# A pre-LN transformer block on one core: transposes of the second LayerNorm placed later, weights of the last block loaded in another order

## The chip, the cores and the metric

The kernel runs on one core of one Trainium2 chip. The metric is the device time of one execution in microseconds (us). A profiled execution is a separate run; its own time stands beside its span below.

## The reference

The inputs are `x` [1, 2048, 512] and the weights, all float32. What is computed, cut to the core:

```python
def A(x, wq, wk, wv, wo):            # 32 query heads of 16, one key/value head
    q = (x @ wq).reshape(B, S, 32, 16).transpose(0, 2, 1, 3)
    k, v = x @ wk, x @ wv
    p = softmax(einsum("bhqd,bkd->bhqk", q, k) * 16 ** -0.5)
    o = einsum("bhqk,bkd->bhqd", p, v)
    return o.transpose(0, 2, 1, 3).reshape(B, S, 512) @ wo

def B(x, w_gate, w_up, w_down):      # 512 -> 1792 -> 512
    return (gelu(x @ w_gate) * (x @ w_up)) @ w_down

h  = x + A(layernorm(x), wq, wk, wv, wo)
h2 = h + B(layernorm(h), w_gate, w_up, w_down)
```

## The kernel before

**Tiling.** The 2048 rows are four blocks of 512 (`NB = 4`, `T = 512`), each of four tiles of 128 rows (`TB = 4`). float32 operands are split into a high and a low part (`hi`, `lo`), and a product is the three terms high-high, high-low and low-high. A prologue normalizes `x` and makes keys, values and the first queries. Then a loop runs over block, group of four heads and key chunk: `scores` (L343) makes two heads' scores on TensorE and their exps `p` on ScalarE, and `weigh` (L356) multiplies exps by values into `acc`. A set of weighings that stand together is a "run of V" (move `v`). `p` tiles live in five buffers (`PB = 5`).

**Weaving.** From a little into block 1 on, the dense work of the block before is woven between the scores: the output projection `pp`, the second LayerNorm, its transposes `pxt`, the gate and up products `pg` and `pu`, and the down products `pd`. These products run on halves of 64 rows, two at a time, in three PSUM banks that `take_bank` hands out in turn (`spare`). The order of TensorE, GpSimd and ScalarE is as written out everywhere (a manual schedule); in the woven part that of VectorE and of the SP queue too. A table of moves, `CYCLES`, gives each round: first `before`, then `finish(count)`, which issues a run of V, then scores (`s`), dense steps (`d`) and further V (`v`). A counter `clock` counts one for each score and dense step and four for each `v`.

**The second LayerNorm.** When a tile's `pp` is done, `norm` (L549) takes the statistics on VectorE (L130, L131) and GpSimd (L133, L134), and `scale` writes the normalized rows `xb` (L554) and notes the clock in `scaled_at`. `before` (L1039) issues a tile's transposes (`turn`, L570) when the clock is `LAG = 6` past that. `turn` makes four TensorE transposes into a PSUM bank (L575), two copies to `x2h` and `x2l` on VectorE (L583, L584), and the load of a later row of `x` into the freed `xb` buffer (L514). The first gate product of a block waits until four tiles are turned.

**Weights.** The split gate and up weights lie in DRAM as `w1`, 512 KB for one product, and go through three buffers; `load_w1` (L493) asks for the one three ahead. The split down weights `w2` come in tiles of 1 MB, seven to a block, also in three buffers (`load_w2`, L502). Both are issued on the SP queue.

**The last block.** `last_dense` (L788) does block 3's dense work with nothing woven beside it, whole products of 12 matmuls at L772. It takes three `p` buffers for `x`, the normalized rows and `h` (`xp`, `xn`, `h`; loads at L810). The last heads' output goes through DRAM: `oT` is copied from `acc` (L371), stored to `acc_d` (L372), loaded to `oc` (L382), and `piece` (L400) divides it on VectorE (L387, L404) ahead of the last quarter of `pp` (L825). `rest` (L777) holds two down products of block 2 as filler between the steps. Behind this, `up` (L863) asks for two `w1` after both of its products, and the loop over `RUNS` asks for two `w2` at the first feature chunk of each run. In this part only the order of TensorE, GpSimd and ScalarE is written out; a scheduler places the DMAs of the SP queue.

Of the kernel before, what the change touches and what calls it, by code (L numbers as in the profile page):

```python
# [10 lines left out]
F32R = mybir.dt.float32r  # L11
# [8 lines left out]
P = 128  # L20
# [6 lines left out]
PB = 5  # L27
# [11 lines left out]
SUMS = ((0, 1, 2, 3), (4, 5, 6, 7), (8, 9, 10, 11, 12, 13))  # L39

LAG = 6

CYCLES = (
    (3, "ssdddddsdddsddds", "vssvssvs"),
# [11 lines left out]
def kernel(  # L56
# [19 lines left out]
    T = 512  # L76
# [77 lines left out]
    def run(outer, first):  # L154
# [271 lines left out]
                pieces[b] = TB  # L426

        late = ExitStack()
        db = None

        def part_weights(pw):

# [67 lines left out]
            w1s[b, f, k] = w  # L500

        def load_w2(b, j):  # L502
            w = db.tile([P, 2, 2, D], F32R, tag="w2", bufs=3, name=f"w2_{b}_{j}")
            nc.sync.dma_start(
                w.bitcast(F32), w2_d[2 * j : 2 * j + 2].rearrange("f p i d -> p f i d").bitcast(F32)
            )
            w2s[b, j] = w
# [10 lines left out]
        tanhs, later = [], []  # L518
        clock = 0

        def prime():
            for i in range(3):
                load_x(i)
                load_w1(i)
            for j in range(3):
                load_w2(0, j)
# [13 lines left out]
        def project(b, t):  # L540
            def terms():
                o_hi, o_lo = o_blk[b]
                sl = slice(t * P, (t + 1) * P)
                return product_terms([
                    (None, (o_hi[:, c, sl], o_lo[:, c, sl]), (wo_hi[:, c, :], wo_lo[:, c, :]))
                    for c in range(DC)
                ])

            def norm():  # L549
                x = xbs[b, t]  # L550
                scaled = layer_norm(db, x, hs[b, t], f"2_{b}_{t}")

                def scale():
                    scaled()  # L554
                    scaled_at[b, t] = clock

                later.insert(min(1, len(later)), scale)

            def done(a, bank):
                if a == 0:  # L560
                    h = db.tile([P, D], F32, tag="h", bufs=6, name=f"h_{b}_{t}")
                    nc.vector.tensor_tensor(h, bank, xbs[b, t], op=ALU.add)
                    hs[b, t] = h
                else:
                    nc.vector.tensor_tensor(hs[b, t], hs[b, t], bank, op=ALU.add)
                    later.append(norm)

            return f"pp_{b}_{t}", 3 * DC, terms, done, lambda: pieces.get(b, 0) > t

        def turn(b, t):  # L570
            tag, bank = take_bank(f"pxt_{b}_{t}")
            pt = bank.rearrange("p (c q) -> p c q", c=DC)
            xn = xbs.pop((b, t))
            for c in range(DC):
                nc.tensor.transpose(pt[:, c, :], xn[:, c * P : (c + 1) * P], ident)  # L575
            if t == 0:
                xTs[b] = [
                    db.tile([P, DC, T], F32R, tag=f"x2{w[0]}", bufs=1, name=f"x2{w[0]}_{b}")
                    for w in ("hi", "lo")
                ]  # L580
            sl = slice(t * P, (t + 1) * P)
            hi, lo = (x[:, :, sl] for x in xTs[b])
            nc.vector.tensor_copy(hi, pt)  # L583
            nc.vector.tensor_tensor(lo, pt, hi.bitcast(F32), op=ALU.subtract)  # L584
            spare.append(tag)
            load_x(b * TB + t + 3)
            turned[b] = t + 1
# [200 lines left out]
        def last_dense():  # L788
            b = NB - 1
            o_hi, o_lo = o_blk[b]  # L790
            xns, hb = {}, {}
            xT_hi = db.tile([P, DC, T], F32R, tag="x2h", bufs=1, name=f"x2h_{b}")
            xT_lo = db.tile([P, DC, T], F32R, tag="x2l", bufs=1, name=f"x2l_{b}")

            def x_turn(t):
                pt = tail_bank(f"pxt_{b}_{t}").rearrange("p (c q) -> p c q", c=DC)
# [11 lines left out]
            )  # L808
            for t in range(TB):
                nc.sync.dma_start(xp[:, t, :], x_t[:, b * TB + t, :])  # L810

            pps = [psum1(f"pp_{b}_0")]
            pps.extend(tail_bank(f"pp_{b}_{t}") for t in range(1, TB))
# [14 lines left out]
                    )  # L828

            def norm(t):  # L830
                scaled[t] = layer_norm(db, xns[t], pps[t], f"2_{b}_{t}", on_act=True)

            piece, scaled = last_out.pop(), {}
            for t in range(TB):
# [26 lines left out]
                nc.scalar.activation(hb[t], pps[t], AF.Copy)  # L861

            def up(f, gh, gl):  # L863
                terms = []
                for k in range(2):
                    w = w1s.pop((b, f, k))
                    terms.append(
                        [(w[:, i, c, :], xT_hi[:, c, :]) for c in range(DC) for i in range(2)]
                        + [(w[:, 0, c, :], xT_lo[:, c, :]) for c in range(DC)]
                    )  # L870
                pg, pu = yield from solo([f"pg_{b}_{f}", f"pu_{b}_{f}"], terms)
                g = db.tile([P, T], F32, tag="g", bufs=2, name=f"g_{b}_{f}")
                nc.vector.tensor_copy(g, pg)
                a = db.tile([P, T], F32, tag="ga", bufs=2, name=f"ga_{b}_{f}")
                nc.vector.tensor_tensor(a, g, g, op=ALU.mult)
                nc.vector.scalar_tensor_tensor(  # L876
                    a, a, 1.0 / GELU_A, g, op0=ALU.add, op1=ALU.mult
                )
                nc.scalar.activation(a, a, AF.Tanh, scale=GELU_A * GELU_C)  # L879
                nc.vector.scalar_tensor_tensor(a, a, 1.0, g, op0=ALU.add, op1=ALU.mult)  # L880
                nc.vector.tensor_tensor(a, a, pu, op=ALU.mult)
                split(nc.vector, gh[:, f % 2, :], gl[:, f % 2, :], a)
                for k in range(2):
                    load_w1(b * 2 * FC + 2 * f + k + 3)

            def down(fs, last):
                for t0 in range(0, TB, 2):
# [20 lines left out]
            for fs in RUNS:  # L908
                early_f = 2 if fs is RUNS[-1] else 1
                for n, f in enumerate(fs):  # L910
                    if f % 2 == 0:
                        gs[b, f // 2] = [
                            db.tile([P, 2, T], F32R, tag=tag, bufs=3, name=f"{tag}_{b}_{f // 2}")
                            for tag in ("gh", "gl")
                        ]
                    yield from up(f, *gs[b, f // 2])
                    if fs is RUNS[-1] and n == 0:
                        load_w2(b, f // 2)
                    if n + 1 == early_f and prev is not None:
                        yield from down(prev, False)  # L920
                    if fs is not RUNS[-1] and n + 1 == early_f:
                        for g in fs[::2]:
                            load_w2(b, g // 2)
                prev = fs
            yield from down(prev, True)

# [48 lines left out]
        with tc.manual_schedule(engines={mybir.EngineType.SP, mybir.EngineType.DVE}):  # L975
            parts = None
            if first:
                work = later_q()
                parts = part_weights(early.enter_context(tc.tile_pool(name="parts", bufs=1)))


            normed = True

            def visit():
                nonlocal work, normed
                total, k = 0, None
                while work is not None and total < 6 and (k != 2 or last == 0):
                    last, k = k, next(work, None)
                    if k is None:
                        work = None  # L990
                        return
                    total += k
                normed = k != 4

            def norm():
                nonlocal normed
                if not normed:
                    next(work)
                    normed = True

            def pace():
                nonlocal n, parts, db
                if n == 2 * PER:
                    drain()
                    for _ in parts or ():
                        pass
                    parts = None
                    early.close()
                    db = late.enter_context(tc.tile_pool(name="dense", bufs=1))
                score(n)  # L1010
                n += 1
                if n % 4:
                    return
                if outs:
                    take_out()
                if parts is not None and n > 12 and n % 24:
                    next(parts, None)
                if n == 2 * PER + 4:
                    prime()

            moves = {"s": pace, "p": visit, "n": norm, "v": partial(finish, 1)}
            for move in OPENING + PERIOD * (PER // KC):
                moves[move]()
            while n < lead:
                pace()
                if n % 4 == 2 and len(pend) > 2 and n < lead - 1:
                    finish(1)
                elif n % 4 == 0:
                    finish(len(pend) - 2)
# [9 lines left out]
        def before(idle):  # L1039
            if outs:  # L1040
                take_out()
            while (b_t := divmod(sum(turned.values()), TB)) in scaled_at:
                if clock - scaled_at[b_t] < LAG:
                    break
                turn(*b_t)
                if not idle:
# [378 lines left out]
```

## Time and profile before

| | |
|---|---|
| time, median of 3 runs | 1445.45 us (1445.38 to 1445.54) |
| the profiled execution: its own time, its span | 1446.27 us, 1444.3 us |
| TensorE matmul (PE) busy | 1397.6 us |
| ScalarE (ACT) busy | 1031.0 us |
| VectorE (DVE) busy | 640.4 us |
| GpSimd (POOL) busy | 218.7 us |
| granted TensorE clock, mean | 0.998 |
| moved by DMA | 180.57 MB |

All times in the profile are in us from the first instruction, so the span lies a little under the execution's time. PE is the matmul row and PEld the weight loads, which overlap it. A row of the timeline has start, length, engine, line, operation, output and input tiles and the count of merged instructions; in brackets stands the idle time of that engine just before and what ended it. A row of the waits has the waiting engine and line, the releaser, the sum, the number of times and the longest. A row of the windows has the stretch and its length, then busy time and instructions of PE, PEld, DVE, ACT and POOL, the granted TensorE clock, the busy share of the 16 DMA engines and GB/s. The chain is the work that ended last, followed back from the end. SPq is the queue of DMAs that the sync engine issues.

### The profile page before, as it was taken

What the parts mean: (1) busy time and instruction counts of PE and PEld (TensorE: products, weight loads), DVE (VectorE), ACT (ScalarE), POOL (GpSimd) and SP (SyncE); (2) the same over time, 40 slices, a digit from 0 to 9 for tenths busy, and PEclk for the clock granted to TensorE, in tenths of its full rate; (3) what the DMA queues carried; (4) which work ended last, traced back from release to release, by engine and by line L of the source; (5) the groups of instructions that cost most, each with busy time, mean ns of one, the idle gap of its engine ahead of it and who ended that gap; (6) DMA issues with size and microseconds to landing.
All of it is one profiled execution on the core that took longest, in us unless ns stands there. A gap on an engine that the chain in (4) does not pass through costs nothing.

```text
span 1444.3 us, 25110 instructions
## 1 busy us (share of the span) xinstructions
PE 1397.6 (97%) x10384; PEld 754.3 (52%) x10384; DVE 640.4 (44%) x1043; ACT 1031.0 (71%) x1147; POOL 218.7 (15%) x305
## 2 busy tenths in 40 slices
PE   6999999999999999998999999998999999999998
PEld 5433333334455555554555555544555555567776
DVE  7413131223364444554354544545264453546665
ACT  7699999996878777785777777786778777752000
POOL 5577778601000000000000000000000000001000
PEclk9999999999999999999999999999999999999999
DMA  4467667633222333211422323211323323224552
GB/s 155 144 212 220 222 222 245 208 133 132 78 95 75 118 100 114 100 56 58 169 82 78 129 100 114 100 49 40 139 93 100 114 99 113 90 88 175 188 176 76
DMA packets 66930, 180.57 MB, mean 125 GB/s; under 512 B 9436, under 2 KB 9436, under 8 KB 66776
## 3 DMA queue, kind: packets, MB, share of 16 engines
q1 hardware_dynamic: 56976, 144.79, 29.8%
q0 software_dynamic: 9760, 34.08, 7.1%
q8 instruction: 84, 1.38, 0.4%
q14 instruction: 38, 0.31, 0.1%
q10 hardware_dynamic: 72, 0.00, 0.0%
HBM read 131.13 MB, written 47.71 MB: 124 GB/s over the span
## 4 chain that ended last, share of the span: by engine, by line
PE 86%; DVE 6%; ACT 3%; DMA 2%; issue 1%; POOL 1%; SPq 0%; ACTq 0%; DVEq 0%; POOLq 0%
PE acc L358 31%; PE s L350 19%; PE pg L742 8%; PE pd L742 7%; PE pu L742 6%; PE pq L203 3%; PE pd L772 3%; ACT p L354 3%; PE pu L772 2%; PE pg L772 2%; PE pp L742 2%; DMA w<-w_d 1%; PE pd_rest L784 1%; DVE st L130 1%; PE pxt L575 0%
## 5 line engine op out<-in xcount | busy, mean ns | idle before, releaser
L354 ACT ACTIVATE p<-s 128x1024 f32<-128x1024 f32 x1024 | 960.5, 1040 | 254.5 <-PE s L350 254.2
L358 PE MATMUL acc<-p,v_sb 128*32 128x512 f32 x4096 | 491.6, 600 | 0.0
L350 PE MATMUL s<-qg,kaug 50*128 50x512 f32 x1984 | 388.2, 426 | 4.1 <-ACT p L354 3.5
L350 PEld LDWEIGHTS s<-qg,kaug 50*128 50x128 f32 x1984 | 171.5, 184 | 284.1 <-issue 133.8
L358 PEld LDWEIGHTS acc<-p,v_sb 128*32 128x32 f32 x4096 | 110.2, 109 | 231.3 <-issue 215.9
L742 PE MATMUL pg<-x2h,w 64*128 64x512 f32 x672 | 177.4, 394 | 4.2 <-DVE g L616 3.1
L742 PE MATMUL pu<-x2h,w 64*128 64x512 f32 x672 | 175.3, 394 | 0.0
L133 POOL TENSOR_SCALAR rstd<-mv 128x1 f32<-128x1 f32 x16 | 3.5, 220 | 989.7 <-DVE mv L131 956.8
L742 PE MATMUL pd<-w,gh 64*128 64x512 f32 x624 | 124.9, 394 | 1.4 <-DVE h L672 1.4
L672 DVE TENSOR_TENSOR h<-h,pd 128x512 f32<-128x512 f32 x80 | 54.3, 685 | 151.7 <-PE pd L742 151.7
L742 PEld LDWEIGHTS pg<-x2h,w 64*128 64x128 f32 x672 | 96.1, 186 | 20.5 <-DVE g L616 6.6
L742 PE MATMUL pg<-x2l,w 64*128 64x512 f32 x336 | 100.7, 392 | 0.0
L742 PEld LDWEIGHTS pu<-x2h,w 64*128 64x128 f32 x672 | 94.3, 186 | 11.2
L742 PE MATMUL pu<-x2l,w 64*128 64x512 f32 x336 | 99.2, 392 | 0.0
L879 ACT ACTIVATE ga<-ga 128x512 f32<-128x512 f32 x14 | 8.9, 632 | 94.5 <-DVE ga L876 94.5
L742 PEld LDWEIGHTS pd<-w,gh 64*128 64x128 f32 x624 | 68.9, 186 | 12.8 <-DVE h L672 2.7
L742 PE MATMUL pd<-w,gl 64*128 64x512 f32 x312 | 72.1, 392 | 0.0
L387 DVE RECIPROCAL oc<-oc 128x128 f32<-128x128 f32 x64 | 56.6, 922 | 32.0 <-DMA oc<-acc_d 31.9
L616 DVE TENSOR_TENSOR g<-g,pg 128x512 f32<-128x512 f32 x42 | 28.8, 685 | 91.1 <-PE pg L742 91.1
L616 DVE TENSOR_TENSOR u<-u,pu 128x512 f32<-128x512 f32 x42 | 28.9, 688 | 78.9 <-PE pu L742 78.7
L612 DVE COPY g<-pg 128x512 f32<-128x512 f32 x42 | 29.0, 691 | 74.2 <-PE pg L742 74.2
L123 DVE CAST qh<-pq 128x512 fp32r<-128x512 f32 x11 | 7.6, 689 | 110.1 <-PE pq L203 110.1
(242 smaller groups left out, 1479.2 us busy)
## 6 DMA issues: line engine op xcount, KB each, us to landing
w<-w_d SPq DMA_DIRECT2D x112, 512.0 KB
w<-w_d SPq DMA_DIRECT2D x28, 1024.0 KB
qg<-q_d SPq DMA_DIRECT2D x62, 200.0 KB
q_d<-qh SPq DMA_DIRECT2D x32, 256.0 KB
acc_d<-oT SPq DMA_DIRECT2D x32, 256.0 KB
oc<-acc_d SPq DMA_DIRECT2D x128, 64.0 KB
w_d<-w_0b POOLq DMA_DIRECT2D x14, 512.0 KB, 3.6
w_d<-w_1b POOLq DMA_DIRECT2D x14, 512.0 KB, 5.2
```

Of the source, the lines that this page charges most:

```text
L130: nc.vector.bn_stats(st, src)
L203: nc.tensor.matmul(pq, wt[:, d, c * P : (c + 1) * P], xt[:, d, :], start=(n == 0), stop=(n == 3 * DC - 1),)
L350: nc.tensor.matmul(s[:, a, :], kaug[rows, kc * P : (kc + 1) * P], qg[rows, u, :], start=True, stop=True,)
L354: nc.scalar.activation(p[:, 2 * u : 2 * u + 2, :], s, AF.Exp, scale=SCALE)
L358: nc.tensor.matmul(acc[32 * j : 32 * j + 32, :], v_sb[:, kc, :], p[:, j, :], start=(kc == 0), stop=(kc == KC - 1), skip_group_check=True,)
L387: nc.vector.reciprocal(oc[:, 1, sl], oc[:, 1, sl])
L612: nc.vector.tensor_copy(half, bank)
L616: nc.vector.tensor_tensor(half, half, bank, op=ALU.add)
L672: nc.vector.tensor_tensor(hs[b, t], hs[b, t], bank, op=ALU.add)
L742: nc.tensor.matmul(bank, lhsT[r], rhs[r], start=(k == 0), stop=(k == n - 1), skip_group_check=True,)
L772: nc.tensor.matmul(bank, lhsT, rhs, start=(i == 0), stop=(i == len(ts) - 1))
L784: nc.tensor.matmul(bank, lhsT, rhs, start=(i == 0), stop=(i == len(ts) - 1))
```

## The change

- The transposes wait for `SETTLE = 14` counts of the clock behind the scaling, where they waited for `LAG = 6`. `LAG` also sets how far the second half of the rows runs behind the first; that stays at 6.
- In the last block, `load_w1` is called after each of the two products of a chunk instead of twice after both.
- In the last block, the first two `w2` tiles lie in the two `p` buffers that are free there, and are asked for right behind the loads of `x`. The other five are asked for behind chunks 1, 2, 5 and 8.
- `x2h` and `x2l` of block 0 are allocated ahead of the other dense tiles, and the small tiles of the LayerNorm in a pool of their own (`tiny`) behind them, so that the dense tiles have other places in SBUF.

```diff
+SETTLE = 14
...
         def load_w2(b, j):
-            w = db.tile([P, 2, 2, D], F32R, tag="w2", bufs=3, name=f"w2_{b}_{j}")
+            if b == NB - 1 and j < 2:
+                w = sb.tile([P, 2, 2, D], F32R, tag="p", bufs=PB, name=f"w2_{b}_{j}")
+            else:
+                w = db.tile([P, 2, 2, D], F32R, tag="w2", bufs=3, name=f"w2_{b}_{j}")
...
+        def new_xT(b):
+            xTs[b] = [
+                db.tile([P, DC, T], F32R, tag=f"x2{w[0]}", bufs=1, name=f"x2{w[0]}_{b}")
+                for w in ("hi", "lo")
+            ]
+
         def prime():
+            new_xT(0)
...
-                scaled = layer_norm(db, x, hs[b, t], f"2_{b}_{t}")
+                scaled = layer_norm(tiny, x, hs[b, t], f"2_{b}_{t}")
...
             for t in range(TB):
                 nc.sync.dma_start(xp[:, t, :], x_t[:, b * TB + t, :])
+            for j in range(2):
+                load_w2(b, j)
...
             def up(f, gh, gl):
-                terms = []
+                banks = []
                 for k in range(2):
                     w = w1s.pop((b, f, k))
-                    terms.append(
-                        [(w[:, i, c, :], xT_hi[:, c, :]) for c in range(DC) for i in range(2)]
-                        + [(w[:, 0, c, :], xT_lo[:, c, :]) for c in range(DC)]
-                    )
-                pg, pu = yield from solo([f"pg_{b}_{f}", f"pu_{b}_{f}"], terms)
+                    terms = [(w[:, i, c, :], xT_hi[:, c, :]) for c in range(DC) for i in range(2)]
+                    terms += [(w[:, 0, c, :], xT_lo[:, c, :]) for c in range(DC)]
+                    banks += yield from solo([f"p{'gu'[k]}_{b}_{f}"], [terms])
+                    load_w1(b * 2 * FC + 2 * f + k + 3)
+                pg, pu = banks
...
-                for k in range(2):
-                    load_w1(b * 2 * FC + 2 * f + k + 3)
...
-                    if fs is RUNS[-1] and n == 0:
-                        load_w2(b, f // 2)
                     if n + 1 == early_f and prev is not None:
                         yield from down(prev, False)
-                    if fs is not RUNS[-1] and n + 1 == early_f:
-                        for g in fs[::2]:
-                            load_w2(b, g // 2)
+                    for j in {1: (2,), 2: (3,), 5: (4,), 8: (5, 6)}.get(f, ()):
+                        load_w2(b, j)
...
                     db = late.enter_context(tc.tile_pool(name="dense", bufs=1))
+                    tiny = late.enter_context(tc.tile_pool(name="tiny", bufs=1))
...
             while (b_t := divmod(sum(turned.values()), TB)) in scaled_at:
-                if clock - scaled_at[b_t] < LAG:
+                if clock - scaled_at[b_t] < SETTLE:
                     break
```

More of the change, by code (lines that the diff above doesn't have):

```diff
@@ L428, in run @@
         late = ExitStack()
-        db = None
+        db = tiny = None
         def part_weights(pw):
@@ L575, in turn @@
                 nc.tensor.transpose(pt[:, c, :], xn[:, c * P : (c + 1) * P], ident)
[L576 to L580, printed above, removed]
+            if b not in xTs:
+                new_xT(b)
             sl = slice(t * P, (t + 1) * P)
@@ L791, in last_dense @@
             xns, hb = {}, {}
-            xT_hi = db.tile([P, DC, T], F32R, tag="x2h", bufs=1, name=f"x2h_{b}")
-            xT_lo = db.tile([P, DC, T], F32R, tag="x2l", bufs=1, name=f"x2l_{b}")
+            new_xT(b)
+            xT_hi, xT_lo = xTs[b]
             def x_turn(t):
@@ L830, in norm @@
             def norm(t):
-                scaled[t] = layer_norm(db, xns[t], pps[t], f"2_{b}_{t}", on_act=True)
+                scaled[t] = layer_norm(tiny, xns[t], pps[t], f"2_{b}_{t}", on_act=True)
             piece, scaled = last_out.pop(), {}
@@ L1001, in pace @@
             def pace():
-                nonlocal n, parts, db
+                nonlocal n, parts, db, tiny
                 if n == 2 * PER:
```

## The prediction

> **What bounds the kernel now.** I read the page first (busy shares, chain by line), then the busy time by stage, then the waits and the order of time around the steps that the change moves.
>
> ```profile
> span 1444.3 us, 25110 instructions
> PE 1397.6 (97%) x10384; PEld 754.3 (52%) x10384; DVE 640.4 (44%) x1043; ACT 1031.0 (71%) x1147; POOL 218.7 (15%) x305
> PE 86%; DVE 6%; ACT 3%; DMA 2%; issue 1%; POOL 1%; SPq 0%; ACTq 0%; DVEq 0%; POOLq 0%
> 500.00:700.00 200.00, 194.05 (x1612) 105.52 (x1608) 93.20 (x151) 148.61 (x162) 3.12 (x8) 1.00 0.26 86
> 700.00:900.00 200.00, 198.22 (x1650) 108.42 (x1644) 94.92 (x144) 152.39 (x167) 0.00 (x0) 1.00 0.33 113
> 900.00:1100.00 200.00, 191.59 (x1564) 102.27 (x1564) 93.35 (x153) 147.38 (x162) 3.12 (x8) 1.00 0.27 91
> ```
>
> TensorE sets the time: 97% busy, 86% of the chain. In the middle, where attention scores and dense products are woven, ScalarE has a quarter of its time free (152 of 200 us), VectorE half. The stretch 700 to 900 loses 1.8 us of TensorE; the stretches with a second LayerNorm (500 to 700, 900 to 1100) lose 6.0 and 8.4. So the LayerNorm costs TensorE something, and what it costs stands in the wait in front of the transposes `pxt`.
>
> ```profile
> who waited for it (us, times):
>   PE pxt L575: 13.8, 10
> 339.83 0.66 PE L575 MATMUL pxt<-ident,xb 128*128 128x128 f32 x4 [2.13 <-DVE xb L554]
> 357.31 0.66 PE L575 MATMUL pxt<-ident,xb 128*128 128x128 f32 x4
> 983.13 0.66 PE L575 MATMUL pxt<-ident,xb 128*128 128x128 f32 x4 [1.54 <-DVE h L562]
> 998.55 0.40 PE L350 MATMUL s<-qg,kaug 50*128 50x512 f32 x2
> 999.98 0.55 DVE L554 TENSOR_SCALAR xb<-h,mv,rstd 128x512 f32<-128x512 f32 x1 [0.99 <-POOL rstd L134]
> 1000.58 0.66 PE L575 MATMUL pxt<-ident,xb 128*128 128x128 f32 x4 [1.64 <-DVE xb L554]
> 1003.57 5.60 ACT L354 ACTIVATE p<-s 128x1024 f32<-128x1024 f32 x6 [3.40 <-PE s L350]
> 1004.02 0.69 DVE L562 TENSOR_TENSOR h<-pp,xb 128x512 f32<-128x512 f32 x1 [0.17 <-PE pp L742]
> 1005.70 0.69 DVE L565 TENSOR_TENSOR h<-h,pp 128x512 f32<-128x512 f32 x1 [0.99 <-PE pp L742]
> 1008.92 0.66 PE L575 MATMUL pxt<-ident,xb 128*128 128x128 f32 x4 [0.90 <-DVE xb L554]
> PEld acc L358 <- ACT p L354: 14.1, 50, 0.3
> L358 PE MATMUL acc<-p,v_sb 128*32 128x512 f32 x4096 | 491.6, 600 | 0.0
> ```
>
> The rows are in order of time, with the idle time ahead of an instruction and what ended it in brackets. The normalized rows `xb` are ready at 1000.53, 1.6 us after the last scores ahead of the transposes, and TensorE, whose order is written out, stands still. That adds up to 13.8 us in ten of the twelve tiles, 0.90 to 2.13 each.
>
> **Part 1: the transposes one run of V later.** Nothing is added or removed. In the built order of the changed kernel each `pxt` of tile t stands where that of tile t+1 stood (in block 0, tiles 1 and 2 stand together, and tile 3 stays); no other TensorE instruction moves, so no round without dense work is added. The new place is about 8.4 us further on (1000.58 to 1008.92), and `xb` is written then. What else could hold the transposes there? Their PSUM bank: of three, two are in the running products and the transpose takes the third. At the place of 1008.92 this is the bank that the addition at 1005.70 has emptied by 1006.4; the wait on `h` at 983.13, which is a wait for a bank, was at a place that no transpose has any more. VectorE's two copies behind each transpose move with it; it has half its time free. The next product takes another bank, and the first gate product comes a round after the last transpose. On the SP queue the load of a row of `x`, issued behind each transpose, moves to behind a store of `oT`, four loads of `oc`, two of `qg` or a store of `h`, which therefore come no later. One such load is needed soon, that of tile 3 of the same block: it is now issued at about 992 in place of 984, and its reader is the addition at 1004.02.
>
> So the whole 13.8 us can go: a transpose without a wait costs its 0.66 us and no gap (357.31). What is late next is ScalarE: V runs now begin earlier against the exps. The weighings are 4096 matmul records, at 24 a run (three weighings, the most that stand together) 171 runs. 14.1 us of waits for exps over 171 runs is 0.08 us a run, for the ten runs that lose their stall 0.8 us. I take 13.8 - 0.8 = **13.0 us gained**. ScalarE idles 3.40 us behind such a place, so it is no new bound. Bounds: 10 if each of the ten meets the longest wait of that row, 0.3 us, and keeps a little of its own; 14.5 if the pipeline's refill behind each stall goes too.
>
> **Part 2: weights of the last block.** Asking for `w1` product by product changes nothing: before, too, each load already waited for its own product only, and the queue order of the `w1` loads is the same. What moves is `w2`: tiles 0 and 1 go into two `p` buffers that the V run at 1280.83 frees, in the SP queue behind `xp`; so tiles 2, 3, 4 take the places that 0, 1, 2 had, and the two loads that were issued together at 1355.93 vanish from there. The pair at 1390.54 stays.
>
> ```profile
> 1323.26 0.43 SPq L504 DMA_DIRECT2D w<-w_d  x1
> 1355.93 1.77 SPq L504 DMA_DIRECT2D w<-w_d  x2
> 1390.54 1.75 SPq L504 DMA_DIRECT2D w<-w_d  x2
> 1360.13 6.31 DMA w<-w_d
> 1366.57 3.02 PE pu L772 x12
> 1369.59 2.79 PE pg L772 x12
> PE pu L772 <- DMA w<-w_d: 2.3, 3, 1.1
> ```
>
> At 1360.13 a `w1` load needs 6.31 us because 2 MB of `w2` lie ahead of it; two products cover 5.6. TensorE ends the waiting product at 1369.59; without the wait it would end three products of 2.79 behind 1360.13, at 1368.5. So **1.1 us gained**. The other two of the three waits keep their causes, `w2` loads at 1323.26 and 1390.54, and remain. Bounds: 0, and 3.0 if all three went: 2.3 in the last row, and 0.2 each for the product that starts slowly (3.02 in place of 2.79).
>
> **Part 3: what the early `w2` tiles stand in front of.** This is the cost. The new SP order is `xp`, `w2` tile 0, two stores of `h`, `w2` tile 1, and only then the last store of `oT` and the loads of `oc`, which everything at the end hangs on.
>
> ```profile
> 1280.83 2.78 PE L358 MATMUL acc<-p,v_sb 128*32 128x512 f32 x24
> 1281.99 1.76 SPq L810 DMA_DIRECT2D xp<-in_A_x_dram  x4
> 1289.76 1.37 SPq L674 DMA_DIRECT2D out_dram<-h  x2
> 1292.68 2.06 DMA acc_d<-oT
> 1296.06 2.25 DMA oc<-acc_d
> 1298.49 0.95 DVE L387 RECIPROCAL oc<-oc 128x128 f32<-128x128 f32 x1 [5.84 <-DMA oc<-acc_d]
> 1306.21 0.50 PE L825 MATMUL pp<-wo_hi,o_hi 128*128 128x512 f32 x1 [0.21 <-DVE o_hi L123]
> 1317.00:1319.00 2.00, 2.00 (x11) 1.60 (x10) 0.69 (x1) 0.83 (x2) 0.00 (x0) 1.00 1.01 383
> ```
>
> Tile 0 is issued right behind `xp`, at 1283.8, and is through before the store at 1292.68 (`xp` and it, 2 MB, are 5.5 us at the 383 GB/s of the last row). Tile 1 stands behind the stores of `h`, issued until 1289.76 + 1.37 = 1291.1, so it goes 1.5 us ahead of the `oT` store. Its 1 MB takes 2.7 us at that rate, of a stretch in which such loads ran; the store's data then wait 2.7 - 1.5 = 1.2 us in the same 16 queues, and I add 0.6 us because the load starts behind the `h` stores. So `oc`, the pieces on VectorE and the last projection come 1.8 us later; TensorE waits for the pieces (0.21 at 1306.21), so there is no slack: **1.8 us lost**. Bounds: 0.5, if the load gets ahead in the pause before the store, and 5.5, if tile 0 too is late and 1 MB + 0.5 MB + 1 MB lie ahead (2.6 MB at 383 GB/s is 6.8 us, less 1.5 of lead, rounded up for their starts).
>
> The Trainium skill ("DMA: Bandwidth & Descriptors", "Anatomy of one DMA") says that DMA engines do not wait on semaphores, they just consume their queues, which speaks against this part; by its fit of 2 us plus bytes over 436 GB/s, 1 MB would hold the queue 2.4 us, and the loss would be an estimated 1.5 us.
>
> **Part 4: order of tiles in SBUF.** No instruction changes, and no row of the trace tells one place in SBUF from another, so I cost the move at 0, with -0.5 and +0.5 as bounds. The early loads of block 0 still lie on buffers whose readers end before 315.
>
> **Sum.** -13.0 - 1.1 + 1.8 = -12.3. The profiled execution took 1446.27 us (span 1444.3 and 2.0 around it), 0.8 above the median 1445.45 of unprofiled runs: 1434.0 profiled, **1433.2 us** as a run.
>
> **Rivals.**
> *The stall moves instead of going.* The V runs, now earlier, wait for exps, or the copies behind a transpose hold the next bank. For it: a stall lets ScalarE catch up. Against it: ScalarE idles 3.40 us right behind. If half the gain is lost, 1433.2 + 6.5 = 1439.7; if all, 1446.2, which is no change.
>
> *The `oT` store is held for longer.* 5.5 us in place of 1.8, and TensorE idle for that long drops its clock. The trace has one such drop:
>
> ```profile
> 304.00:308.00 4.00, 3.05 (x24) 0.93 (x16) 1.37 (x4) 3.86 (x6) 1.28 (x4) 1.00 0.10 24
> 308.00:312.00 4.00, 3.88 (x18) 0.78 (x19) 0.00 (x0) 2.82 (x4) 0.00 (x0) 0.59 0.17 62
> 303.73 1.92 PE L358 MATMUL acc<-p,v_sb 128*32 128x512 f32 x16
> 308.55 3.52 PE L358 MATMUL acc<-p,v_sb 128*32 128x512 f32 x16
> ```
>
> The same 16 matmuls took 3.52 in place of 1.92 us, so a drop costs 1.6. That gives 1433.2 + 3.7 + 1.6 = 1438.5. The Trainium skill ("TensorE: Matmul & The Clock Gate", "Part 1: The HAM clock gate") puts the drop behind an idle window of about 3.4 us; the drop above came behind a stretch that was 76% busy, so the trace is the stricter one.
>
> *Slower: the `oT` store behind slow loads.* The same place with another price. All that stands ahead of the store from 1283.8 on, 2.6 MB, would have to move at the rate that the queues show there today:
>
> ```profile
> 1285.00:1291.00 6.00, 5.46 (x40) 3.25 (x41) 3.25 (x5) 3.02 (x4) 0.00 (x0) 1.00 0.31 102
> ```
>
> At 102 GB/s it is through at 1309.5, and the store, whose data would have started near 1293.6, is 15.9 us late; with one drop of the clock, 1433.2 - 1.8 + 15.9 + 1.6 = 1448.9. It decides from a delay of 14.1 us (110 GB/s) with no drop, and the change is slower by over 0.2% from 17.0 us, or 15.4 with a drop. Against it: the 102 GB/s are what was asked for, with the engines 31% busy; where more was asked for they moved 383.
>
> *It doesn't do what it says.* For `w1` this is so (part 2). For the transposes the built order shows the move.
>
> **Chances.** Forecast 0.74; stall half kept 0.08, wholly 0.03; store held for longer 0.10; slower 0.05. About 0.2%, 2.9 us, is what a measurement here can tell from no change. Faster by more: 0.74 + 0.08 + 0.10 = 0.92; within: 0.03; slower: 0.05. The range: the low end 1429.5 takes the good ends of part 1 (1.5 more), part 3 (1.3) and some of parts 2 and 4 (0.9); the high end 1439.0 takes in the longer hold.
>
> **What would show it.** In the profile after: no idle time ahead of `pxt` and about 13 us less between the first and the last of the woven rounds; V runs with the same 0.3 us waits; one `DMA w` wait gone near 1366 and two left; `acc_d` landing 3 to 5 us after its issue in place of 2.06, and the reciprocal behind it late by as much. Wrong would be: a new releaser ahead of the V runs, the transposes still waiting, or an `oc` landing over 5 us late with a granted clock under 1.

## The result and the profile after

| | before | after |
|---|---|---|
| time, median (lowest to highest) | 1445.49 us (1445.38 to 1445.78) | 1430.61 us (1429.58 to 1433.01) |
| ratio, with its 95% interval | | 0.9899 (0.9882 to 0.9916) |
| the profiled execution: own time, span | 1446.27 us, 1444.3 us | 1433.01 us, 1430.9 us |

The change takes 14.9 us off; 12.3 were forecast. First the busy time of the kernel after in the three stretches of the middle, in the columns of the windows above, and its waits for exps:

```profile
500.00:700.00 200.00, 199.32 (x1656) 107.73 (x1656) 93.70 (x153) 151.56 (x165) 3.12 (x8) 1.00 0.30 100
700.00:900.00 200.00, 198.20 (x1648) 108.14 (x1650) 95.73 (x146) 153.52 (x169) 0.00 (x0) 1.00 0.30 101
900.00:1100.00 200.00, 196.79 (x1612) 104.60 (x1612) 95.76 (x157) 151.93 (x166) 3.12 (x8) 1.00 0.28 94
PE pxt L587 <- issue: 0.2, 1, 0.2
PEld acc L360 <- ACT p L356: 13.2, 46, 0.3
```

The stretches with a second LayerNorm went from 194.05 and 191.59 to 199.32 and 196.79, the one without stayed. The 13.8 us ahead of `pxt` are 0.2 now, and the runs of V do not wait longer for exps (13.2, before 14.1). In the order of time, a transpose now stands between scores and weighings without a bracket, so without idle time:

```profile
987.77 0.39 PE L352 MATMUL s<-qg,kaug 50*128 50x512 f32 x2
988.09 0.66 PE L587 MATMUL pxt<-ident,xb 128*128 128x128 f32 x4
988.67 1.92 PE L360 MATMUL acc<-p,v_sb 128*32 128x512 f32 x16
```

The stores of `oT` are good clocks, since every group ends with one. The view groups them from 290 us on: count, shortest, median and longest issue, first and last start. First before, then after:

```profile
L372 SPq DMA_DIRECT2D acc_d<-oT x25: 319/320/389, 307.1 to 1292.7; - x25
L374 SPq DMA_DIRECT2D acc_d<-oT x25: 319/320/383, 308.6 to 1279.7; - x25
```

From the first to the last of them it took 985.6 us before and 971.1 after: **14.5 us gained in the woven part**. Up to the first, the profiled execution after lost 1.5. From the last to the end of the span it is 151.6 before and 151.2 after, **0.4 gained in the last block**. 14.5 - 1.5 + 0.4 = 13.4, the difference of the spans.

The 1.5 us are a half clock early in this execution (the granted clock is the third number from the end):

```profile
60.80:62.40 1.60, 1.60 (x12) 0.16 (x8) 1.00 (x2) 1.52 (x2) 0.00 (x0) 0.62 0.57 197
62.40:64.40 2.00, 2.00 (x12) 0.70 (x12) 0.00 (x0) 1.21 (x2) 1.87 (x2) 0.50 0.52 193
```

Nothing that the change moves has run by then, and a kernel below that holds the whole change (the gap of 256 bytes) has its first store in this view at 307.2, where before had it at 307.1. The profiled execution is also the longest of the four after; so the step from profile to profile is 13.3 us and that of the medians 14.9.

In the last block two things moved against each other. The chain there, in order of time, kernel after:

```profile
1279.69 4.97 DMA acc_d<-oT
1296.02 0.96 PE pp L836 x3
1306.98 2.72 PE pg L781 x12
1315.17 6.07 DMA w<-w_d
1321.38 3.00 PE pu L781 x12
1335.26 11.21 PE pd L781 x48
1368.27 10.88 PE pd L781 x48
1381.90 6.89 DMA w<-w_d
1408.25 16.33 PE pd L781 x72
PE pu L781 <- DMA w<-w_d: 2.2, 2, 1.6
```

and the same products in the kernel before:

```profile
1320.06 2.79 PE pu L772 x12
1346.10 11.20 PE pd L772 x48
1380.75 11.14 PE pd L772 x48
1421.14 16.81 PE pd L772 x72
```

The store of `oT` takes 4.97 us in place of 2.06, and the last quarter of the projection follows it by 16.33 us in place of 13.53. Of the three `w1` waits that near 1366 is gone, the other two are there, and their sum is 2.2 in place of 2.3. And nearly all weight products of this block are quicker: twelve take 2.72 us in place of 2.79, 72 take 16.33 in place of 16.81, though no instruction of theirs has changed. Only the first product of 48 is as slow as before, 11.21 us.

### The profile page after: what moved, and what is told of

Same layout as the page of the kernel before. It is cut to its first block, busy times and chain, and to the rows that moved or that the text cites. A ratio compares the mean times of both kernels' runs of the same rounds, so it can differ in the third digit from the quotient of the medians.

```text
span 1430.9 us, 25109 instructions
## 1 busy us (share of the span) xinstructions
PE 1396.5 (98%) x10384; PEld 752.4 (53%) x10384; DVE 639.4 (45%) x1043; ACT 1031.6 (72%) x1147; POOL 219.4 (15%) x305
## 4 chain that ended last, share of the span: by engine, by line
PE 89%; DVE 4%; ACT 3%; DMA 1%; issue 1%; SPq 0%; ACTq 0%; DVEq 0%
PE acc L360 31%; PE s L352 19%; PE pg L751 8%; PE pd L751 8%; PE pu L751 7%; PE pq L205 4%; ACT p L356 3%; PE pd L781 3%; PE pp L751 2%; PE pu L781 2%; PE pg L781 2%; DMA w<-w_d 1%; PE pk L1219 1%; PE pd_rest L793 1%; DVE ga L644 0%
## 5 line engine op out<-in xcount | busy, mean ns | idle before, releaser
L751 PEld LDWEIGHTS pu<-x2h,w 64*128 64x128 f32 x672 | 94.7, 185 | 11.4
```

The source lines that it names most:

```text
L751: nc.tensor.matmul(bank, lhsT[r], rhs[r], start=(k == 0), stop=(k == n - 1), skip_group_check=True,)
```

## The experiments

**Part 1 alone.** The kernel before with one number changed:

```diff
+SETTLE = 14
...
-                if clock - scaled_at[b_t] < LAG:
+                if clock - scaled_at[b_t] < SETTLE:
```

> The kernel before with the later transposes alone. Theory: the stall in front of the transposes goes whole, and its refill with it. The stores of oT, one for each round of heads, stand 14.5 us closer together across the three LayerNorm stretches in the changed kernel (3.2, 5.5 and 5.6), so 1445.5 - 14.5 = 1431.0, and the last block takes as long as before: 12 gate matmuls in 2.79 us, the last oT store lands in 2.1 us, three waits for w1. Rival: part of the 14.5 is due to the other places of the tiles (a faster pitch in the woven products too); then 1432 to 1436, with idle time ahead of the transposes gone all the same.

Measured: 1431.16 us (1427.34 to 1432.18), ratio to before 0.9882 (0.9866 to 0.9899). So part 1 by itself brings what the whole change brings. Its stores of `oT`, and its two rows of waits:

```profile
L374 SPq DMA_DIRECT2D acc_d<-oT x25: 319/320/388, 307.0 to 1278.6; - x25
PE pxt L577 <- issue: 0.2, 1, 0.2
PEld acc L360 <- ACT p L356: 13.6, 49, 0.3
```

The woven part takes 971.6 us, 14.0 less than before, with no shift ahead of it, and the tiles are in their old places, so the rival of the expectation is out.

**Places in SBUF alone.** The kernel before with part 4 only:

```diff
         def prime():
+            new_xT(0)
...
-                scaled = layer_norm(db, x, hs[b, t], f"2_{b}_{t}")
+                scaled = layer_norm(tiny, x, hs[b, t], f"2_{b}_{t}")
```

> The kernel before with the other order of tiles in SBUF alone. In the changed kernel 12 gate or up matmuls of the last block took 2.72 us in place of 2.79, and 72 down matmuls 16.33 in place of 16.81. Theory P (place): where the operands lie sets that pitch, so it comes with this edit alone: 28 products x 0.07 + 0.3 + 0.5 for the down products = 2.8 us less, 1442.7; stalls at the transposes as before, 13.8 us. Rival L (loads): the pitch follows the traffic of the loads; then 2.79 stays and the time is 1445.5.

Measured: 1442.14 us (1441.66 to 1446.1), ratio 0.9975 (0.9962 to 0.9987): faster by 3.8 us of the medians, which is theory P: the place sets the pace, and the loads do not. From the last store of `oT` to the end it is 1440.2 - 1292.2 = 148.0 us in place of 151.6. The chain of its last block:

```profile
1319.44 2.72 PE pu L776 x12
1345.30 10.88 PE pd L776 x48
1378.38 10.88 PE pd L776 x48
1417.57 16.33 PE pd L776 x72
```

**Loads of the last block alone.** The kernel before with parts 2 and 3 (`w2` tiles 0 and 1 in two `p` buffers and asked for early, the rest behind chunks 1, 2, 5 and 8, `w1` product by product), its tiles in the old places:

```diff
+            if b == NB - 1 and j < 2:
+                w = sb.tile([P, 2, 2, D], F32R, tag="p", bufs=PB, name=f"w2_{b}_{j}")
...
+            for j in range(2):
+                load_w2(b, j)
```

> The kernel before with the last block's loads alone (w1 asked for product by product, two w2 tiles early in p buffers). The last oT store lands 5.0 us after its issue in place of 2.1 (+2.9), one of three waits for w1 goes (-1.1). Theory P: the pitch stays 2.79, in all 1445.5 + 1.8 = 1447.3. Rival L: the pitch falls to 2.72, 1444.5.

Measured: 1448.62 us (1446.92 to 1450.03), ratio 1.0014 (1.0004 to 1.0023): slower by 2.0 us by the ratio and 2.7 by the medians, and again P. The store of `oT` is held as in the kernel after, and the matmuls have their old pace:

```profile
1294.08 4.80 DMA acc_d<-oT
1372.42 2.80 PE pg L780 x12
1422.78 16.75 PE pd L780 x72
```

What these loads gain in `w1` waits (0.4 us in one, before 2.3 in three) is about what they cost at the store: from the last store of `oT` to the end it is 151.7 us, before 151.6. What makes the kernel slower is therefore not in the last block as its profile shows it; 1.4 us stand ahead of its first store in the view of the stores, with the same early drop of the clock as after. Whether these loads make that drop more frequent stays open, and so does the rest.

**One early tile in place of two.** The kernel after, with only `w2` tile 0 in a free `p` buffer; tile 1 goes into the dense pool and is asked for behind chunk 1:

```diff
-            if b == NB - 1 and j < 2:
+            if b == NB - 1 and j < 1:
...
-            for j in range(2):
-                load_w2(b, j)
+            load_w2(b, 0)
...
-                    for j in {1: (2,), 2: (3,), 5: (4,), 8: (5, 6)}.get(f, ()):
+                    for j in {1: (1, 2), 2: (3,), 5: (4,), 8: (5, 6)}.get(f, ()):
```

> The changed kernel with one w2 tile early in place of two, so that no weight load stands between the stores of h and the last oT store. Theory: tile 1 was what held that store; it lands in 2.1 us again, and the pieces come 2.9 us earlier; tile 4 is asked for during the first down products and may make one w1 wait of up to 0.4 us. 1430.6 - 2.9 + 0.2 = 1427.9. Rival: the store was held by tile 0, issued right behind the loads of x, which still is early: then it lands in 4 to 5 us as in the changed kernel, and the time is 1430.6 or more.

Measured: 1427.36 us (1426.24 to 1428.66), ratio 0.9862 (0.9845 to 0.9878). The store is free again, and one `w1` wait is left:

```profile
1279.63 2.09 DMA acc_d<-oT
PE pu L781 <- DMA w<-w_d: 1.2, 1, 1.2
1331.49 11.18 PE pd L781 x48
1364.43 10.88 PE pd L781 x48
```

So tile 1 is what held the store. From the last store of `oT` to the end it is 147.0 us in place of 151.2, and the kernel is quicker than the kernel after (ratio to before 0.9862 against 0.9899, with intervals that do not meet).

**What in the place counts.** In the built programs `x2h` and `gh` start 256 bytes past a multiple of 512 before, `w1` and `w2` 384; after, all four start at 384. (These places are those of the built programs; no trace shows an address.) Three kernels move them:

```diff
+            gap = db.tile([P, 32], F32, name="gap")
+            nc.vector.memset(gap, 0.0)
```

stands behind `x2h` and `x2l` for 128 bytes (with 64 in place of 32 for 256 bytes), or among the constants, where it shifts all of the pool.

> The kernel after, with a tile of 128 bytes a partition put between the turned hidden state (x2h, x2l) and all the other tiles of its pool: x2h stays where it was, w1, w2 and gh lie 128 bytes further on. Theory R (a matmul is quicker where its moving and its stationary tile start at the same place within 256 or 512 bytes): the twelve matmuls of a gate or up product go back from 2.72 to 2.79 us, since x2h and w1 now differ by 128 bytes; the down products of 48 and 72 stay at 10.88 and 16.33, since w2 and gh move together. Theory A (each tile's own place counts, and 384 bytes past a multiple of 512 is a good one): the gate and up products, with w1 moved off that place, and the down products, with both moved off it, all go back, to 2.79, 11.14 and 16.81. By R the part from the last oT store to the end gets 28 x 0.07 = 2.0 us longer than in the kernel after (151.17), by A 28 x 0.07 + 0.26 + 0.48 and as much again for the other half of the rows, some 3.5.

> The same with a tile of 256 bytes: x2h lies 384 bytes past a multiple of 512, w1, w2 and gh 128 past one. Theory R by 256 bytes: 2.72 for twelve gate or up matmuls, 10.88 and 16.33 for 48 and 72 down matmuls, the last block as in the kernel after (151.17 us from the last oT store). Theory R by 512 bytes: 2.79 for the gate and up products, 10.88 and 16.33 for the down products. Theory A: 2.79, 11.14 and 16.81.

> The kernel after with a tile of 128 bytes among the constants, so that x2h, w1, w2 and gh all lie 128 bytes further on, at a multiple of 512. Theory R: nothing changes, 2.72, 10.88 and 16.33 us for 12, 48 and 72 matmuls. Theory A (384 past a multiple of 512 is the good place): 2.79, 11.14 and 16.81.

From the chain of each, gap of 128 bytes first, then 256, then all shifted:

```profile
1305.89 2.79 PE pg L783 x12
1368.36 10.90 PE pd L783 x48
1407.64 16.38 PE pd L783 x72
```

```profile
1305.75 2.72 PE pg L783 x12
1366.96 10.88 PE pd L783 x48
1406.22 16.33 PE pd L783 x72
```

```profile
1304.47 2.72 PE pg L783 x12
1365.33 10.88 PE pd L783 x48
1404.35 16.33 PE pd L783 x72
```

That is theory R by 256 bytes: a gate or up product is slow when `w1` lies 128 bytes off `x2h`, as quick as ever when it lies 256 off; the down products, whose two operands moved together, do not care; and shifting everything changes nothing. One run each, so their times (1432.36, 1431.5 and 1429.26) say little, but a pace that repeats in 28 products is not chance. The Trainium skill ("SBUF — State Buffer", "Operand start alignment") asks only for a multiple of the element size and adds that this is about legality, not speed; all these places are legal, and the runs show that they differ in speed.

**The buffers of the exponentials, too.** The first down product stays at 11.21 us after and 11.18 in the kernel with one early tile: its `w2` lies in a `p` buffer, 480 bytes past a multiple of 512, where `gh` is at 384. The kernel with one early tile, with 96 bytes at the top of that pool:

```diff
+                    if b == 0:
+                        pad = sb.tile([P, 24], F32, name="pad")
+                        nc.vector.memset(pad, 0.0)
```

> The kernel of e4_one_early (only the first w2 tile in a free buffer of the exponentials) with a tile of 96 bytes at the top of the attention's pool, so that the buffers of the exponentials lie 384 bytes past a multiple of 512 as w1, w2 and gh do, not 480. Theory R and theory A: the first down product, whose first w2 tile lies in such a buffer, goes from 11.18 us for 48 matmuls towards 10.88; half of its matmuls have that tile, and it runs twice, so some 0.3 us come off the last block (146.98 from the last oT store) where the cost lies on those matmuls alone, 0.6 where it lies on all 48. The attention's own matmuls move a tile at 384 against a stationary one at 160, before 480 against 160: congruent in neither case, so nothing by R, and the 32 stores of oT come when they came. Time 1427.0, 1426.5 to 1427.4.

Measured: 1426.3 us (1426.15 to 1426.5), ratio 0.9863 (0.9846 to 0.9879), the quickest kernel here by its median.

```profile
1329.74 10.88 PE pd L784 x48
300.00:320.00 20.00, 18.70 (x134) 5.82 (x126) 4.65 (x9) 19.68 (x23) 1.34 (x4) 1.00 0.31 103
PE pu L784 <- DVE g L886: 0.8, 1, 0.8
PE pu L784 <- DMA w<-w_d: 0.7, 2, 0.5
```

The product went to 10.88, 0.3 us. (The expectation counted that piece of 48 twice; it runs once.) In the kernel with one early tile only half of the 48 matmuls read the `p` buffer, and yet all of 0.30 us were lost; why the other half is slow too was not tried. The medians differ by 1.1 us, but they come from two sessions, and by the ratio to before the two kernels are alike (0.9862 and 0.9863). The profiles differ in the clock too: with the padding the drop at 308 us is missing, granted 1.00 over 300 to 320 where before, after and the kernel with one early tile have 0.91. The padding is not its cause, since the last kernel below has the padding and 0.91. The wait of 0.8 us, at 1382, is put down to VectorE's copy of a gate sum (`g`).

**The cause of the `w1` waits.** The kernel after without four of its `w2` loads; the down products read tile 2 in their place, so its output is not the block's:

```diff
         def load_w2(b, j):
+            if b == NB - 1 and j > 2:
+                w2s[b, j] = w2s[b, 2]
+                return
```

> The kernel after without the loads of w2 tiles 3 to 6 of the last block: its down products read tile 2 in their place (left out: those four loads, so the down sums of features 6 to 13 are of other weights). Theory L: the w1 waits of the last block, 2.2 us in two pieces after, come from w1 loads that share the DMA engines with the w2 loads asked for beside them; both go, to under 0.3 us, and the last block gets about 2 us shorter, 149 from the last oT store to the end. Theory W: a w1 tile that is asked for two products ahead of its use is late by itself; the waits stay, at 1 us or more in all, and the last block stays within 0.7 us of 151.17.

One run, 1427.14 us. The waits of TensorE from 1300 on are an empty list; from the last store of `oT` to the end it is 1425.0 - 1276.9 = 148.1 us in place of 151.2. So theory L: a `w1` load is late here only where `w2` loads go with it. Each wait costs its length and another 0.28 us, since the product behind it takes 3.00 in place of 2.72.

**More lead for `w1`.** The kernel with the padding, with one more buffer for `w1` in the last block:

```diff
+            if b == NB - 1 and m == 3:
+                w = sb.tile([P, 2, 2, DC, P], F32R, tag="p", bufs=PB, name=f"w1_{b}_{f}_{k}")[:, 0]
...
-                    load_w1(b * 2 * FC + 2 * f + k + 3)
+                    for m in (3, 4) if f == k == 0 else (2 * f + k + 4,):
+                        load_w1(b * 2 * FC + m)
```

> The kernel of e7_attn96, with the second w1 tile of feature 1 of the last block in the free buffer of the exponentials, and with that every later w1 tile asked for one product earlier, four products ahead. If the w1 waits come from the time between asking and use, whatever shares the engines, they go: none of more than 0.3 us in place of 0.7 in two pieces; the last block gets some 0.7 us shorter and the time 1425.6, 1425.0 to 1426.3. If what ends the wait is the order on SP (a w1 tile behind two w2 tiles), 1426.3 stays. If the early tile falls onto the store of oT, that store takes over 3 us instead of 2.06 and the time is 1427 or more.

Measured: 1426.8 us (1425.33 to 1427.08), ratio 0.9865 (0.9848 to 0.9881): no gain. The two early waits went; at the same product that waited 0.8 us for `g`, TensorE now waits 1.8, for `w1`:

```profile
1371.79 1.73 SPq L515 DMA_DIRECT2D w<-w_d  x2
1375.87 7.05 DMA w<-w_d
PE pu L787 <- DMA w<-w_d: 1.8, 1, 1.8
```

Two `w2` tiles, 2 MB, are issued 2.4 us ahead of that `w1` tile, which lands 7.05 us after its issue. But this tile had no more lead than without the edit, though the expectation counts on it. After the tile in the `p` buffer (issued at 1300.52), the loads of `w1` follow the ends of the first three products of the block (issues at 1305.15, 1307.87 and 1310.59), skip the end of the fourth, and go on behind the fifth (1316.03). The next buffer still holds a tile that has to be read, so that from there on each load is again three products ahead of its use. The edit gave more lead to these four tiles alone, and there the waits went. Whether more lead, or an order that puts `w1` ahead of the two `w2` loads, would end the late wait was not tried; nor were two `w2` loads spread apart.

## Why the prediction was right, and where its terms were off

| step | forecast, us | measured, us |
|---|---|---|
| part 1, transposes | -13.0 (-10 to -14.5) | -14.5; alone -14.0 |
| part 2, `w1` waits | -1.1 (0 to -3.0) | -0.4 |
| part 3, store of `oT` | +1.8 (+0.5 to +5.5) | +2.9 |
| part 4, places | 0 (-0.5 to +0.5) | -2.8 in the last block |
| clock drop in the profiled execution | not in the sum | +1.5 |

They add up to -13.3, the step from profile to profile. The prediction had the mechanism of parts 1 to 3; its size was off in each of them, and part 4 was put at nothing.

**Part 1** was right in mechanism and in size to within 1.5 us. The step that was off is the deduction: 0.8 us were taken off for runs of V that meet later exps. The row of those waits fell instead, 14.1 to 13.2, and to 13.6 with part 1 alone. The stall's 13.6 plus that fall gives 14.5 and 14.1, what the stores say. That is not proof that the row has this price: with the places alone it falls to 11.4, and only 0.8 us come off the woven part. The profiles do not resolve such differences either. With the later transposes, the woven part took 970.6 to 971.6 us in the five profiles that have the drop of the clock at 308 us, as before has it, and 968.3 to 969.7 in the four without. Against 985.6 before, the five give a gain of 14.0 to 15.0, more than the 13.6 of the stall; whether the rest is this row or the refill of the pipeline behind a stall, which the prediction took for its bound of 14.5, stays open. The rival in which the stall moves to the exps is out.

**Part 2** named the right wait and the right two that stay. The term was too large since the two that stayed did not keep their size: 2.2 us in two in place of 2.3 in three. The gain is 0.1 and one slow start, some 0.25. With the loads alone, at the old pace, one wait of 0.4 us was left; so the quicker products of part 4 may have met later loads and given some of their gain back here, which no run shows by itself. That `w1` product by product changes nothing was argued from the order of the loads; by itself it was not tried.

**Part 3** put the cost at the right place, behind tile 1, and 1.1 us too low. The term that was off is the rate. It was 383 GB/s, from a stretch with a dense queue of loads; here the queues moved

```profile
1278.00:1284.00 6.00, 6.00 (x34) 4.22 (x24) 0.69 (x1) 0.00 (x0) 0.00 (x0) 1.00 0.87 285
```

from the issue of tile 1 at 1278.25 on, and next to nothing in the microsecond behind it. That is 1.7 MB, tile 1 and the store of `oT` (1.25 MB) and the rest of the stores of `h`. At 383 GB/s the same bytes would have been through 1.5 us earlier; the store landed at 1284.66. The estimate by the Trainium skill ("DMA: Bandwidth & Descriptors", "Anatomy of one DMA"), 1.5 us, was further off; that section gives its fit for the path of DMAs issued by GpSimd, and these are issued on SP. Neither 5.5 nor 15.9 us, and the clock stayed at 1.00 throughout:

```profile
1270.00:1300.00 30.00, 27.18 (x132) 17.47 (x125) 13.81 (x30) 5.66 (x7) 3.32 (x10) 1.00 0.41 140
```

So the rival with the longer hold and a drop of the clock is out, and the slower one with it.

**Part 4** was the step that failed: its mechanism was not in the prediction at all. No row of the trace told one place from another, and the bounds of 0.5 us were drawn as if that were a proof. The last block before has a single pace, 2.79 us for twelve and 11.14 to 11.20 for 48, and nothing there hints that 2.72 was to be had. 28 gate and up products by 0.07 are 1.96 us; the second and third down products gave 0.26 and 0.48, the filler `pd_rest` 0.06. The misses in the last block, +1.1 at the store, +0.7 at the `w1` waits and -2.8 here, ran against each other. With part 4 at its forecast of 0 the median would have been some 2.8 us higher, 1433.4, close to the forecast 1433.2; that would have been luck as well, since the 1.5 us more of part 1 would then have stood against the 1.8 of parts 2 and 3. The forecast of part 1, which carries the result, was right for its reason.

## What to carry to other kernels

When an in-order engine stands still for a value that another engine is about to finish, count the length of the stall over all its places, and look for a later place with nothing new to wait for: this one number was worth 14 us, more than all the rest together. Early loads into free buffers are not free when a small transfer on the path follows them on the same queue; ask for the one that fits into the pause, and leave the other. And when tiles change places, compare the pace of the unchanged matmuls.

## What the runs showed of the hardware

A matmul of 128x128 on 128x512 in these float32 terms takes 227 ns (2.72 us for twelve) where its moving and its stationary tile start at the same place or 256 bytes apart, counted within 512, and 233 ns (2.79) where they start 128 bytes apart. A product of 48 with all or half of its moving tiles 96 bytes off took 11.21 and 11.18 us in place of 10.88. In the woven part, with halves of 64 rows two at a time, the time was 984.8 us with the new places alone and 985.6 before, one profile each.

The granted clock can halve for 3 to 4 us at the same place of a kernel in one execution and not in another: at 61 us in five of the twelve profiles here (after, the loads alone, one early tile, the gap of 128 bytes, all shifted), and at 308 us in six (before, after, part 1 alone, one early tile, the gap of 256 bytes, more lead for `w1`). With the places alone and with the loads alone a drop lies between 330 and 350 us instead. The early drop goes with a shift of the first store by 1.5 us, the one at 308 us with the 1 to 3 us between the two groups of woven parts above. The four runs of the kernel after lie 3.4 us apart. What sets a drop off was not tried.
